# Seven tiles of k and q loaded eight tokens to a packet and turned by products, a first mask added by TensorE, and priorities by kind of work

## The chip, the cores and the metric

The kernel runs on one core of one Trainium2 chip. Its time is the device time of one execution in microseconds (us), the median of several runs. A core has five engines that matter here: PE (TensorE, products; PEld is its weight load), DVE (VectorE), ACT (ScalarE), POOL (GpSimd) and SP (SyncE, which here only issues transfers). Sixteen DMA engines move data between memory (HBM) and the on-chip SBUF. Products are written to PSUM, which has eight banks.

## The reference

Attention with four sink tokens and a window of 128, and a gated feed-forward network over its result:

```python
def _attn_ref(q, k, v, n_sink, window):          # q, k, v: (4, 8, 768, 64) float32; n_sink 4, window 128
    scores = np.matmul(q, k.transpose(0, 1, 3, 2)) / np.sqrt(D)
    keep = (pos[None, :] < n_sink) | ((rel >= 0) & (rel < window))     # rel = query - key
    scores = np.where(keep, scores, -1e9)
    a = softmax(scores)
    return np.matmul(a, v)

def _moe_ref(x, w_gate, w_val, w_out, rms_g):    # x: 3072 tokens x 512; d_ff 1536
    xn = x / np.sqrt(np.mean(x * x, axis=-1, keepdims=True) + 1e-6) * rms_g
    g = xn @ w_gate
    return (g * sigmoid(g) * (xn @ w_val)) @ w_out                     # float32
```

x is the attention's output with the eight heads side by side in a row of 512.

## The kernel before

**Tiles.** The 4 x 768 tokens are 24 tiles of 128 tokens, six to a batch; tile `bt` has index `t` within its batch. For each tile k, q and v (256 KB each in float32) are loaded by three transfers issued on SP (`load`, L415) into a ring of nine buffers `st`. A partition holds one token, and each of its eight heads is a run of 64 floats, 256 bytes, in memory. `casts` makes bfloat16 of them (`so` for k and q, with the scale in q's; `V` for v). `qk_unit` turns k and q, so that the head dimension lies on the partitions (`KQT`): for tiles 0 to 11 by four PE transposes of 128x128 for each tensor and a copy out of PSUM (L471, L476), from tile 12 on by a DMA transpose. On the first tile of a batch it also copies the sinks' k (`KS`), and on the others it makes the scores with the sinks (L491).

**Visits.** A tile has two visits of four heads (`visit`). The scores (L545, four products of 64 rows) go to a pair of banks, or two single ones; DVE masks them there, takes the negated maximum (L587), and ACT takes four exponentials (L591). On a batch's first tile the mask is a predicated copy of -1e30 over the keys after the query (L558, `m_first`, `negbig`); on other tiles the older tile's scores are copied over the current tile's where the window has moved on (L567, `m_old`), and the sinks' scores are put beside them (L578, and L597 and L601 for their exponentials). The weights are turned by PE (L609, the first twelve visits) or by DMA transposes, POOL splits them into the current and the older tile's part (L625, L629), and products with V follow (L638 for the sinks, L646, L651), with a reciprocal (L662) and the division into `x` (L665) on DVE.

**Rows and network.** `rows` normalizes a tile (ACT L675, POOL L677, L680 and L683, DVE `xr` L323) and turns it (`xnt`: PE L696 for the first tiles, then DMA transposes). `f_unit` makes a gate product and a value product (L721, sixteen matmuls of 128 columns for the first four tiles and the last two, which stand alone; eight of 256 for the others, which go in pairs, each unit then covering two column blocks), a tanh on ACT (L735), and two DVE products (`p` L739, `h` L742). `o_unit` makes the output (L753, twelve matmuls of 512 columns in three parts), copied by ACT (L764) and stored by SP (L767).

**Weights.** Nine transfers of 512 KB in bfloat16, read as float32 from memory, are issued by POOL: gate and value columns in three parts each (L441, g0 to g2 and v0 to v2), then the output weights (L447). `FIRST` gives their order and earliest time in the plan. The first of them waits until k of tile 1 has landed (`HOLD`).

**Order.** Nothing is left to a scheduler at run time. `Plan.order` simulates all operations with the written costs and due times, takes at each step the one that can start first and, among those, the one of lowest rank, chooses engine and bank for it, and the kernel is written out in that order for each engine (`add_manual_dep`). Every engine works in its order, so an instruction that waits holds up all behind it on its engine. `room` adds some slack after `ROOM_FROM` between an operation's end on one engine and its use on another. Attention runs up to `LEAD` = 12 visits ahead of the network. Where the plan has gaps on PE before 38 us, `Plan.fill` puts in products of a blank tile (L819), each reckoned at 0.109 us, whose result nobody uses.

Of the kernel before, what the change touches and what calls it, by code (L numbers as in the profile page):

```python
# [9 lines left out]
ALU = mybir.AluOpType  # L10
ACT = mybir.ActivationFunctionType
AX = mybir.AxisListType
FP32 = mybir.dt.float32
# [14 lines left out]
FFRANK = 1000.0  # L28
QK_DMA = 12
FIRST = "g0:2 v0:10 g1:13 v1:18 g2:20 v2:27 o1:38 o2:39 o0:39"  # L30
SHARES = {"SP": 0.2, "POOL": 0.95}
ROOM = {"PE": 0.6, "DVE": 0.2}
ROOM_FROM = 70.0
# [25 lines left out]
class Plan:  # L59
# [10 lines left out]
    def op(self, alts, fn, reads=(), writes=(), rank=0.0, takes=None, banks=(), after=()):  # L70
        o = Op(alts, fn, rank)
# [18 lines left out]
    def dma(self, queue, issue, moves, fn, reads=(), writes=(), rank=0.0, lag=1.1, after=()):  # L90

        o = self.op([(queue, issue, issue)], fn, reads=reads, rank=rank, after=after)
# [15 lines left out]
    def order(self):  # L108
# [59 lines left out]
        while len(done) < len(self.ops):  # L168
            pick = None
            for o in ready:  # L170
# [9 lines left out]
                key = (s, o.rank)  # L180
                if pick is None or key < pick[0]:
                    pick = (key, o, c, a)
            t = event()
            if t is not None and (pick is None or t <= pick[0][0]):
# [49 lines left out]
def kernel(  # L234
# [72 lines left out]
    def evac(n):  # L307
        return on(DVE=0.09 + 0.47e-3 * n, ACT=on_act(n))
# [32 lines left out]
    negbig = const.tile([P, 1], FP32, name="negbig")  # L341
    m_old = const.tile([P, P], I16, name="m_old")
    m_first = const.tile([P, P], I16, name="m_first")
# [33 lines left out]
    def c_masks():  # L377

        for m in (m_old, m_first):
            nc.gpsimd.memset(m, 1)  # L380
            nc.gpsimd.affine_select(
                out=m, in_=m, compare_op=ALU.is_gt, fill=0,
                base=0, pattern=[[1, P]], channel_multiplier=-1,
            )
        nc.gpsimd.memset(m_first[:, 0:NS], 0)

    def c_small():
        nc.vector.memset(negbig, NEG)
        nc.vector.memset(nhalf, -0.5)
        for i in range(2):  # L390
            nc.vector.memset(KS[i], 0.0)
        for i in range(10):
            nc.vector.memset(V16[i][:, :, D:D + 1], 1.0)
# [6 lines left out]

    plan.op(on(POOL=0.8), c_ident, writes=["ident"], rank=-3000)
    plan.op(on(DVE=0.6), c_small, writes=["small", ("KS", 0), ("KS", 1)] + [("V", i) for i in range(10)], rank=-3000)
    plan.op(on(ACT=1.4), lambda: nc.scalar.activation(out=warm, in_=nhalf, func=ACT.Exp), reads=["small"], rank=-3000)
    plan.op(on(POOL=1.4), c_masks, writes=["masks"], rank=-2999)
    plan.op(on(DVE=1.2), c_sinks, writes=[("VS", 0), ("VS", 1)] + [("PK", i) for i in range(NPS)], rank=-2999)

# [3 lines left out]
    def load(bt, rank):  # L410

        b, t = divmod(bt, NT)
        for i, src in enumerate((k, q, v)):
            n = (3 * bt + i) % len(ST)
            LOADED[bt, i] = plan.dma("SP", 0.45, 1.33, lambda src=src, n=n: nc.sync.dma_start(  # L415
                out=ST[n], in_=src[b, :, t * P:(t + 1) * P, :].rearrange("h t d -> t h d"),
            ), writes=[("ST", n)], rank=rank + 0.1 * i,
                after=VISIT[2 * bt - PACE:2 * bt - PACE + 1] if 2 * bt >= PACE else [])

    def casts(bt, rank):  # L420

        for i, nm in enumerate("kqv"):
# [12 lines left out]
            plan.op(alts, fn, reads=[("ST", n)], writes=[key], rank=rank + 0.1 * i)  # L435

    def load_w(nm, i, rank):
# [3 lines left out]
        return plan.dma("POOL", 0.78, 3.1 if c1 - c0 > 256 else 1.8, lag=1.5, fn=lambda: nc.gpsimd.dma_start(  # L441
# [3 lines left out]
    def load_wo(part, rank):  # L445
        f0, f1 = 4 * part, 4 * part + 4
        return plan.dma("POOL", 0.78, 3.1, lag=1.5, fn=lambda: nc.gpsimd.dma_start(  # L447
# [5 lines left out]
    def qk_unit(b, t, rank):  # L453
# [6 lines left out]
        if bt >= QK_DMA:  # L460
            plan.dma("SP", 1.2, 1.6, lambda: nc.sync.dma_start_transpose(
                out=KQT[par][:, t].rearrange("c a h p -> c (a h) p"), in_=SO[m].rearrange("p a d -> p (a d)")),
                reads=[("SO", m, 0), ("SO", m, 1)], writes=[("k", par, t), ("q", par, t)], rank=rank)
        else:
            for i, nm in enumerate("kq"):
                bk = Banks(ONES)

# [7 lines left out]
                o = plan.op(on(PE=0.23), tr, reads=["ident", ("SO", m, i)], takes=bk, rank=rank + 0.1 * i, after=after)  # L475
                plan.op(evac(HP * P), lambda e, bk=bk, i=i: copy(  # L476
# [405 lines left out]
```

## Time and profile before

| | us |
|---|---|
| median of 3 runs | 266.91 (266.44 to 267.27) |
| the profiled execution | 267.78 |
| its span, first to last instruction | 266.0 |
| mean granted TensorE clock | 0.999 |

| engine | busy us | share | instructions |
|---|---|---|---|
| PE | 254.8 | 96% | 2685 |
| PEld | 190.1 | 71% | 2702 |
| DVE | 211.0 | 79% | 510 |
| ACT | 147.3 | 55% | 419 |
| POOL | 140.0 | 53% | 272 |

HBM was read at 28.57 MB and written at 6.29 MB; the sixteen DMA engines moved 41.83 MB in 129155 packets, 121312 of them under 512 bytes.

How to read it: the span is cut into 40 slices, and each digit of a slice is the busy share of it in tenths. A group of instructions is given with its line, engine, operation, tiles written and read, count, busy time, mean duration of one in ns, and behind the bar the idle time of its engine just before them and what ended it. Matmuls overlap in the array, so the mean duration of one is longer than the distance between two starts. In windows, each engine's busy time in a stretch is followed by its instruction count, and the last three numbers are the granted clock, the DMA share and GB/s. The chain is the work that ended last, followed back from the end.

### The profile page before, as it was taken

What the parts mean: (1) busy time and instruction counts of PE and PEld (TensorE: products, weight loads), DVE (VectorE), ACT (ScalarE), POOL (GpSimd) and SP (SyncE); (2) the same over time, 40 slices, a digit from 0 to 9 for tenths busy, and PEclk for the clock granted to TensorE, in tenths of its full rate; (3) what the DMA queues carried; (4) which work ended last, traced back from release to release, by engine and by line L of the source; (5) the groups of instructions that cost most, each with busy time, mean ns of one, the idle gap of its engine ahead of it and who ended that gap; (6) DMA issues with size and microseconds to landing.
All of it is one profiled execution on the core that took longest, in us unless ns stands there. A gap on an engine that the chain in (4) does not pass through costs nothing.

```text
span 266.0 us, 7200 instructions
## 1 busy us (share of the span) xinstructions
PE 254.8 (96%) x2685; PEld 190.1 (71%) x2702; DVE 211.0 (79%) x510; ACT 147.3 (55%) x419; POOL 140.0 (53%) x272
## 2 busy tenths in 40 slices
PE   8998998999998999999999999999999999999994
PEld 6686877865666857858758668587587686785981
DVE  3977699999989898988959959679689599494641
ACT  2463676867767647456645467356664555551430
POOL 3566646579446897563637645734534446243100
PEclk9999999999999999999999999999999999999999
DMA  8999999979999989999999969969792431412311
GB/s 162 214 182 210 209 209 199 204 157 233 209 170 165 199 170 187 163 246 192 216 148 240 172 119 226 173 165 179 158 195 40 92 86 25 123 28 46 101 42 39
DMA packets 129155, 41.83 MB, mean 157 GB/s; under 512 B 121312, under 2 KB 125920, under 8 KB 129120
## 3 DMA queue, kind: packets, MB, share of 16 engines
q1 hardware_dynamic: 124368, 36.65, 75.2%
q0 software_dynamic: 4752, 4.72, 10.9%
q8 instruction: 21, 0.34, 0.6%
q14 instruction: 14, 0.11, 0.1%
HBM read 28.57 MB, written 6.29 MB: 131 GB/s over the span
## 4 chain that ended last, share of the span: by engine, by line
PE 81%; DVE 10%; DMA 5%; issue 2%; ACT 1%; POOL 0%; POOLq 0%
PE one L721 45%; PE one L753 22%; DMA wg_bf<-in_moe_w_gate_dram 5%; PE pair L545 4%; PE one L819 3%; DVE nmax L587 3%; PE one L646 2%; PE one L651 2%; PE one L638 1%; PE one L471 1%; DVE one L567 1%; PE one L609 1%; DVE h L742 1%; DVE so L323 1%; DVE x L665 1%
## 5 line engine op out<-in xcount | busy, mean ns | idle before, releaser
L721 PE MATMUL one<-xnt,wg_bf 128*128 128x256 bf16 (+1 forms) x720 | 72.0, 251 | 1.7 <-DMA wg_bf<-in_moe_w_gate_dram 1.0
L721 PE MATMUL one<-xnt,wv_bf 128*128 128x256 bf16 (+1 forms) x720 | 72.2, 251 | 0.3 <-DMA wv_bf<-in_moe_w_val_dram 0.2
L753 PE MATMUL one<-wo_bf,h 128*128 128x512 bf16 x271 | 68.1, 379 | 0.9
L735 ACT ACTIVATE th<-one 128x512 bf16<-128x512 f32 x72 | 42.7, 602 | 42.3 <-PE one L721 35.0
L721 PEld LDWEIGHTS <-wg_bf 128*128 128x128 bf16 x720 | 57.4, 98 | 10.5 <-issue 2.0
L721 PEld LDWEIGHTS <-wv_bf 128*128 128x128 bf16 x720 | 57.3, 98 | 9.7 <-issue 3.2
L739 DVE SCALAR_TENSOR_TENSOR p<-th,one 128x512 bf16<-128x512 bf16 x72 | 48.3, 677 | 15.1 <-ACT th L735 14.8
L591 ACT ACTIVATE ps<-pair,nmax 128x128 bf16<-128x128 f32 x152 | 43.7, 370 | 16.5 <-DVE nmax L587 8.6
L742 DVE TENSOR_TENSOR h<-p,one 128x512 bf16<-128x512 bf16 x72 | 48.3, 679 | 3.3 <-PE one L721 2.1
L753 PEld LDWEIGHTS <-h 128*128 128x128 bf16 x288 | 25.7, 98 | 26.3 <-issue 2.5
L683 POOL TENSOR_TENSOR xg<-x,grow 128x512 bf16<-128x512 bf16 x24 | 27.9, 1165 | 29.5 <-DVE x L665 27.1
L625 POOL TENSOR_SCALAR_AFFINE_SELECT cur<-pt 128x512 bf16<-128x512 bf16 x40 | 25.6, 639 | 29.5 <-DMA pt<-ps 21.5
L764 ACT ACTIVATE osb<-one 128x512 f32<-128x512 f32 x24 | 14.4, 599 | 24.0 <-PE one L753 23.8
L587 DVE TENSOR_REDUCE nmax<-pair 128x4 f32<-128x528 f32 (+1 forms) x38 | 26.5, 696 | 0.5
L567 DVE COPY_PREDICATED pair<-m_old,pair 128x512 f32<-128x512 int16 x32 | 22.0, 688 | 5.0 <-PE pair L545 4.0
L629 POOL TENSOR_SCALAR_AFFINE_SELECT old<-pt 128x512 bf16<-128x512 bf16 x40 | 25.8, 644 | 0.1
L597 POOL TENSOR_TENSOR sd<-sk,nmax 128x16 f32<-128x16 f32 x40 | 8.9, 224 | 25.7 <-DVE nmax L587 23.3
L665 DVE TENSOR_TENSOR x<-one,rden 128x256 bf16<-128x256 f32 x48 | 20.0, 417 | 0.5
L675 ACT ACTIVATE sq<-x 128x512 bf16<-128x512 bf16 x24 | 15.2, 634 | 9.2 <-DVE x L665 7.2
L819 PE MATMUL one<-blank 128*128 128x256 bf16 x132 | 19.2, 295 | 1.2 <-POOL blank L370 1.2
L662 DVE RECIPROCAL rden<-one 128x4 f32<-128x4 f32 x48 | 8.4, 176 | 10.8 <-PE one L651 9.4
L819 PEld LDWEIGHTS <-blank 128*128 128x128 bf16 x132 | 13.4, 106 | 3.8 <-POOL blank L370 1.2
(73 smaller groups left out, 305.2 us busy)
## 6 DMA issues: line engine op xcount, KB each, us to landing
st<-in_k_dram SPq DMA_DIRECT2D x24, 256.0 KB, 4.6
st<-in_q_dram SPq DMA_DIRECT2D x24, 256.0 KB, 4.9
st<-in_v_dram SPq DMA_DIRECT2D x24, 256.0 KB, 5.1
out_dram<-osb SPq DMA_DIRECT2D x24, 256.0 KB, 2.9
wg_bf<-in_moe_w_gate_dram POOLq DMA_DIRECT2D x3, 512.0 KB, 10.5
wv_bf<-in_moe_w_val_dram POOLq DMA_DIRECT2D x3, 512.0 KB, 9.2
wo_bf<-in_moe_w_out_dram POOLq DMA_DIRECT2D x3, 512.0 KB, 10.6
pt<-ps SPq DMA_TRANSPOSE x36, 3.3
```

Of the source, the lines that this page charges most:

```text
L567: nc.vector.copy_predicated(out=ap[:, :, P:2 * P], mask=m_old.unsqueeze(1).to_broadcast((P, hs.stop - hs.start, P)), data=ap[:, :, 0:P],)
L587: nc.vector.tensor_reduce(out=nm[:, hs], in_=ap[:, :, c0:2 * P], axis=AX.X, op=ALU.max, negate=True)
L591: plan.op(on(ACT=0.253), lambda h=h: nc.scalar.activation(out=PSM[r3][:, h, :], in_=head(h)[:, P:2 * P], func=ACT.Exp, bias=nm[:, h:h + 1] ...
L625: plan.op(on(POOL=0.6), lambda: nc.gpsimd.affine_select(out=cur, in_=PTT[r3][:, 0:4, :], compare_op=ALU.is_ge, fill=0.0, base=0, pattern=[ ...
L629: plan.op(on(POOL=0.6), lambda: nc.gpsimd.affine_select(out=old, in_=PTT[r3][:, 0:4, :], compare_op=ALU.is_gt, fill=0.0, base=0, pattern=[ ...
L683: plan.op(on(POOL=1.05), lambda: nc.gpsimd.tensor_tensor(out=xg, in0=X16[r], in1=grow, op=ALU.mult), reads=xs + ["g"], writes=[("XG", bt % ...
L721: nc.tensor.matmul(out=bank(bk)[:, i * n * P:(i + 1) * n * P].rearrange("p (t c) -> p t c", c=P), lhsT=w[:, kt, ft * P:(ft + 1) * P], rhs= ...
L735: plan.op(on(ACT=0.49), lambda: nc.scalar.activation(out=th, in_=b3(gb), func=ACT.Tanh, scale=0.5), banks=[gb], after=[o], writes=[("TH", ...
L739: plan.op(on(DVE=0.6), lambda: nc.vector.scalar_tensor_tensor(out=p1, in0=th, scalar=1.0, in1=b3(gb), op0=ALU.add, op1=ALU.mult,), banks=[ ...
L742: plan.op(on(DVE=0.6), lambda: nc.vector.tensor_tensor(out=HT[g % len(HT)][:, f0:f1, 0:n * P], in0=p1, in1=b3(vb), op=ALU.mult,), banks=[v ...
L753: nc.tensor.matmul(out=bank(bk)[:, 0:DM], lhsT=h[:, ft, tb * P:(tb + 1) * P], rhs=wo_bf[:, ft, :], start=(ft == 0), stop=(ft == FTN - 1),)
L819: done = plan.fill(done, lambda: nc.tensor.matmul(out=ONE[-1][:, 0:256], lhsT=blank[:, 0:P], rhs=blank, start=True, stop=True), 0.109)
```

## The change

1. **Loads.** For tiles 0 to 6 (`WIDE = 7`) k and q are loaded with partition (h, a) holding eight consecutive tokens of head h, 8 x 64 floats, 2 KB to a packet; v stays as it was.
2. **Turning.** For these tiles each tensor is turned by sixteen products with half of the identity's columns, 64 columns each, into a float32 bank (L515 of the new file), and copied out of it with the tokens put back in order (DVE or ACT).
3. **First mask.** `m_first` becomes a bfloat16 tile of 0 and -1e30. On a batch's first tile PE writes it to the scores' banks by two products with the identity (L605), and the scores' products add to it; the predicated copies of L558 and `negbig` are gone. The masks are made by two POOL steps in place of one.
4. **Priorities.** Each operation is given a kind. `place` shifts its rank by `SHIFT`, and by `EARLY` too for early ones; the network's operations have ranks of half their number plus `FEED`. In the plan loads get earliest times (`BEGIN`), weights another order and other times (`FIRST`), the slack is smaller but holds from 40 us on and for all engines, ACT may take an operation of lower rank that starts up to 0.05 us later before 20 us, and the plan's transfer cost of a load is 0.75 or 1.2 in place of 1.33.

In the orders that result, PE has 56 fillers in place of 132, DVE 476 instructions in place of 509; ten of the fourteen turned copies are on ACT; POOL copies more of V; and the first loads on SP are k, q of tile 0, q of tile 1, v of tile 0, k of tile 1.

```diff
+WIDE = 7
-FIRST = "g0:2 v0:10 g1:13 v1:18 g2:20 v2:27 o1:38 o2:39 o0:39"
+FIRST = "g0:5@4 v0:8@5 g1:10@2 v1:20@3 g2:19@6 v2:22@7 o1:37@0 o2:39@1 o0:45@8"
-ROOM = {"PE": 0.6, "DVE": 0.2}
-ROOM_FROM = 70.0
+ROOM = {"PE": 0.3, "DVE": 0.1, "ACT": 0.1, "POOL": 0.4, "SP": 0.1}
+WINDOW = {"ACT": 0.05}
+WINDOW_TO = 20
+SHIFT = {
...
+EARLY = {
...
+FEED = {"gate": 1000, "tanh": 9, "val": 14, "p1": 4, "h": 8, "out": 1000, "out_copy": 1000, "store": 1000}
+BEGIN = {(0, 2): 2, (1, 0): 2, (5, 2): 13, (6, 1): 23, (6, 2): 25, (7, 0): 25, (8, 1): 37, (9, 2): 48}
+ROOM_FROM = 40.0
...
+    def place(self, kind, rank):
+        if rank < -900:
+            return rank
+        if kind in FEED:
+            return (rank - FFRANK) / 2 + FEED[kind]
+        return rank + SHIFT.get(kind, 0.0) + (EARLY.get(kind, 0.0) if rank < 16 else 0.0)
...
-            LOADED[bt, i] = plan.dma("SP", 0.45, 1.33, lambda src=src, n=n: nc.sync.dma_start(
-                out=ST[n], in_=src[b, :, t * P:(t + 1) * P, :].rearrange("h t d -> t h d"),
+            wide = bt < WIDE and i < 2
+            LOADED[bt, i] = plan.dma(f"load_{i}", "SP", 0.45, 0.75 if wide else 1.2, lambda src=src, n=n, wide=wide: nc.sync.dma_start(
+                out=ST[n].rearrange("p j d -> p (j d)") if wide else ST[n],
+                in_=src[b, :, t * P:(t + 1) * P, :].rearrange("h (a j) d -> h a (j d)" if wide else "h t d -> t h d", **({"j": H} if wide else {})),
...
+                def turn(i=i, bk=bk):
+                    for j in range(H):
+                        for r in range(2):
+                            nc.tensor.matmul(
+                                out=bank(bk)[64 * r:64 * r + 64, 64 * j:64 * j + 64], lhsT=SO[m][:, i, D * j:D * j + D],
+                                rhs=ident.rearrange("p (g r a) -> p r g a", g=HP, r=2)[:, r], start=True, stop=True,
+                                skip_group_check=True,
+                            )
+                if bt < WIDE:
+                    o = plan.op("turn", on(PE=0.5), turn, reads=["ident", ("SO", m, i)], takes=bk, rank=rank + 0.1 * i, after=after)
+                    plan.op("turn_out", on(DVE=0.6, ACT=on_act(DM)), lambda e, bk=bk, i=i: copy(
+                        e, KQT[par][:, t, i].rearrange("c g (a j) -> c j g a", j=H),
+                        bank(bk).rearrange("c (j g a) -> c j g a", j=H, g=HP)),
+                        banks=[bk], after=[o], writes=[(nm, par, t)], rank=rank + 0.1 * i)
+                    continue
...
+        def m_mm():
+            for hs, ap in parts():
+                for i in range(0, hs.stop - hs.start, 2):
+                    nc.tensor.matmul(
+                        out=ap[:, i:i + 2, P:2 * P], lhsT=ident, rhs=m_first.unsqueeze(1).to_broadcast((P, 2, P)),
+                        start=True, stop=False, skip_group_check=True,
+                    )
+        if t == 0:
+            first = plan.op("mask_mm", on(PE=0.22), m_mm, takes=sb, reads=["ident", "first"], after=after + VISIT[-1:], rank=rank)
...
-                        start=True, stop=True,
+                        start=(t > 0), stop=True, skip_group_check=(t == 0),
...
-        if t == 0:
-            def mask():
-                for hs, ap in parts():
-                    w = hs.stop - hs.start
-                    nc.vector.copy_predicated(
-                        out=ap[:, :, P:2 * P], mask=m_first.unsqueeze(1).to_broadcast((P, w, P)),
-                        data=negbig.unsqueeze(2).to_broadcast((P, w, P)),
-                    )
```

## The prediction

> **What bounds the kernel now.** I read the page's slices first, then groups by form, then windows, and last the chain and the PE timeline of 19 to 45 us. The page says that PE is full:
>
> ```profile
> span 266.0 us, 7200 instructions
> PE 254.8 (96%) x2685; PEld 190.1 (71%) x2702; DVE 211.0 (79%) x510; ACT 147.3 (55%) x419; POOL 140.0 (53%) x272
> PE   8998998999998999999999999999999999999994
> DMA  8999999979999989999999969969792431412311
> PEclk9999999999999999999999999999999999999999
> ```
>
> PE is above 0.8 everywhere, but part of that does nothing: the plan fills its gaps before 38 us with products of a blank tile, 132 of them in all. The groups by form price them, and what the change touches:
>
> ```profile
> L819 PE MATMUL one<-blank 128*128 128x256 bf16 x132 | 19.2, 295 | 1.2 <-POOL blank L370 1.2
> L471 PE MATMUL one<-ident,so 128*128 128x128 bf16 x96 | 9.2, 223 | 1.3 <-DVE p L739 0.6 <-DVE so L323 0.5
> L558 DVE COPY_PREDICATED_SCALAR pair<-m_first,negbig 128x512 f32 x6 | 4.4, 738 | 0.1
> L558 DVE COPY_PREDICATED_SCALAR one<-m_first,negbig 128x256 f32 x4 | 1.7, 478 | 0.0
> ```
>
> The windows, of all engines, say where the span is lost (PE busy is the third number):
>
> ```profile
> 0.00:19.56 19.56, 17.68 (x166) 13.60 (x167) 13.44 (x55) 8.60 (x26) 10.10 (x29) 1.00 1.05 186
> 19.56:24.90 5.34, 4.10 (x67) 3.21 (x67) 3.86 (x11) 1.00 (x3) 3.00 (x6) 1.00 1.23 211
> 24.90:45.00 20.10, 18.86 (x291) 16.74 (x292) 17.10 (x44) 13.54 (x38) 12.91 (x23) 1.00 1.11 202
> 45.00:90.00 45.00, 42.85 (x548) 31.61 (x546) 43.03 (x121) 33.92 (x102) 28.60 (x57) 1.00 1.14 191
> 90.00:250.00 160.00, 159.37 (x1483) 115.95 (x1492) 127.77 (x275) 86.69 (x247) 85.40 (x161) 1.00 0.80 149
> ```
>
> The same windows for L819 alone give 14.46, 0.28 and 4.42 us of filling in the first three. So PE's time without real work is 16.3 us before 19.56 (1.88 idle, 14.46 filling), 1.5 to 24.90, 5.7 to 45, 2.2 to 90, 0.6 to 250, and 4.0 at the end, 30.3 together; 235.7 us are real. From 90 us on nothing but PE's work sets the time. The loss lies before 45 us, where the chain names the second gate weights:
>
> ```profile
> 12.79 12.07 DMA wg_bf<-in_moe_w_gate_dram
> 24.90 1.07 PE one L721 x16
> 25.97 2.18 PE one L819 x20
> ```
>
> and the timeline shows PE standing there, with filling behind:
>
> ```profile
> 19.56 1.05 PE L721 MATMUL one<-xnt,wg_bf 128*128 128x128 bf16 x16
> 24.90 1.07 PE L721 MATMUL one<-xnt,wg_bf 128*128 128x128 bf16 x16 [1.04 <-DMA wg_bf<-in_moe_w_gate_dram]
> 38.11 1.26 PE L819 MATMUL one<-blank 128*128 128x256 bf16 x10
> ```
>
> So the lever is the moment t2 when the second gate product starts (24.90), and how much attention work PE has behind it by then.
>
> **The change, part by part.** *Loads.* The hardware queue alone moved 1.05 MB in 5 to 10 us: 1.25 us for 256 KB in packets of 256 bytes. The price of 2 KB packets is bounded by two rows: 1.25 (no gain), and the weights' queue, whose packets read 2 KB and were busy 93% of the 16 engines for 750 packets in 15 to 20 us, 99 ns each, so 128 / 16 x 99 ns = 0.8 us. I take 0.8, since packet size is what they share: 0.45 us less for each of fourteen loads. The stalls of SP in its queue (7.98 and 6.43 us at 12.96 and 21.03) should go, as a wide load puts 128 packets there instead of 1024; who was late behind them were casts of tiles 3 and 4.
>
> *Weights.* POOL's first weights follow the VS copy, which needs v of tile 0. That load is now fourth, behind three wide ones: 3 x 0.8 + 1.25 = 3.7 us of transfers, as before (3 x 1.25). The cast of it waits less on DVE (7.37 before, some 6.6 now), so the first gate weights are issued at about 8.3 instead of 9.11. From that issue to the landing of the second gate weights before took 15.8 us, with 1.1 MB of loads beside (10 to 25 us), 4.2 loads; two thirds wide saves 2.8 x 0.45 = 1.3. So they land at about 8.3 + 15.8 - 1.3 = 22.8; with more of the loads done already, 21.5.
>
> *Attention ahead of the first gate.* k of tile 0 lands about 0.4 us earlier, at 3.6. From there to the first xr the new DVE order holds 37 instructions (six casts, three turned copies, five maxima, four masks and so on), 14.2 us by the rows; DVE's instructions start 0.08 us before the one ahead ends, so some 11.8. With 1.2 to 3 us of waits, as in this trace, xr comes at 16.6 to 18.4 (18.05 before), the first gate 1.3 later, and the second 3.1 after that (two units of 0.9, two of L646/L651 at 0.35, scores 0.33, two fillers): 21.0 to 22.8. Both sides agree, and t2 = 22.5.
>
> *What PE has done by t2.* Counting both orders at the trace's spacing (a tensor of L471 0.22, scores 0.33, or 0.22 on a first tile, L609 0.28 or 0.22, products with V 0.35 or 0.13, a unit of L721 0.9): before, six tensors, four scores, four of L609, four products with V and two units, 7.3 us (7.0 by the windows without L819 and idle time). After, at the old prices: eight, eight, five, five and two, 9.1. So 1.8 us of later work is gone by t2.
>
> *Turning by products.* A turned tensor is 16 products of 64 columns for 4 of 128. L646/L651, of 65 columns, start 0.030 us apart, so 0.48; at best two halves of the array run at once (0.24); at worst each waits for its weight load, 98 ns, 1.57. To this comes the change of shape: four scores take 0.33 us at 256 columns and 0.22 at 128, so 0.11 of each group is fixed. By 0.030, the nearest row, and half of the fixed part, 0.55, or 0.33 more than 0.22. Eight fall before t2, where PE waits anyway; six behind it cost 2.0 us.
> The Trainium skill speaks against this form: its page TensorEngine Tiling (Array Packing), Key Properties, says that a change of tiling mode drains the engine, and its Restrictions (Tile-to-Partition Mapping) that column tiling does without fast weight load. By the whole 0.11 at each turned tensor the six would cost 2.2; the trace agrees in that 0.11.
>
> *The first mask.* Two products of 256 columns, 0.22 us a visit at the 0.109 of L721 (16 in 1.74); two visits lie in the gaps, six cost 1.3. DVE loses 6.1 us of L558; 1.6 of them stood at 7.90 to 9.43 on the chain, which is within t2. If the gaps were gone, the first two would cost 0.44. The mask now waits on POOL's m_first, done at about 2.7 us in this trace, and behind it in PE's order stand only fillers and the first turned tensor, whose k lands at 3.6.
>
> *Filling behind t2.* The new order has 56 fillers, ten of them behind the second gate; before, 36 (4.42 us). Ten are 1.3: 3.1 less. This holds only where the work that the plan puts there is ready.
>
> *Queues and copies.* DVE has 33 instructions fewer; ten of the fourteen turned copies and most copies of xnt are ACT's (0.59 for 0.41 us on DVE). ACT was busy 75% in 45 to 90 us and hides them; uncovered, the two on tile 0's way cost 0.4, counted in the waits above. Behind 45 us the relief of DVE could return at most the 2.2 us idle there; the new priorities may as well lose as much. I take 0, with 1 us either way, and none at the end, whose last units stand in the same order.
>
> *Sum.* t2 - 24.9 - 1.8 + 2.0 + 1.3 - 3.1 = t2 - 26.5: -4.0 us at t2 = 22.5. The profiled execution took 267.78, 1.78 around its span, so 263.8 for one like it; the median of the runs is 0.87 lower, 266.91, and gives **262.9**. 0.3% (0.8 us) is about what a measurement of this kernel can tell from no change.
>
> **Rivals.** *The loads gain nothing* (2 KB packets cost as many bytes): g1 still lands at 24.9, t2 - 26.5 = -1.6, 265.3. For it: the 0.8 is another queue's. Against it: that queue reads 2 KB in 99 ns on the same engines. Chance 0.15.
>
> *The weights come later than before.* Place: the DMA engines from 10 to 25 us. In 15 to 20 us the loads got 0.16 MB beside 0.74 MB of weights, packet against packet of an eighth of the size; wide loads have packets as large. If they take as many turns, six wide and three narrow loads pass, 6 x 0.8 + 3 x 1.25 = 8.6 us for 5.3 before, and t2 = 24.1 + 3.3 = 27.4, +0.9, and about 0.5 again at the next weights: 268.3. It decides from t2 = 26.5 on. Against it: the first wide loads are through before the weights start. Chance 0.15, of which 0.03 within 0.3%.
> The Trainium skill (DMA: Bandwidth & Descriptors, Queues, rings and completion order) states this rule: each engine changes rows at packet boundaries. The trace agrees in that 0.16 to 0.74.
>
> *Turning costs the weight load*, 1.57: six behind t2 cost 8.1 for 2.0, eight before it push t2 to about 24.9: +4.5, 271.4. Against it: 30 ns between L646 and L651, which also load weights each time. Chance 0.05.
>
> *The priorities lose the gain behind 45 us* (3 to 4 us of new gaps; 0.05 now in any 10 us): no change, 0.03.
>
> **Chances.** The forecast has the other 0.62; its own range, with t2 from 21.0 to 24.9 and the 1 us, is 259.5 to 265.5. Faster 0.62 + 0.15 = 0.77, same 0.06, slower 0.17. The range over all, 259.5 to 267.6, leaves out the slower cases and 0.03 below.
>
> **What would show it.** Right: gate weights used from 18 us, the second gate at 21 to 24; fillers 56 and about 8 us; turned tensors 0.5 to 0.6 apart; SP without issues of several us; PE idle behind 45 us still 7 us with the end. Wrong: a DMA wait of 2 us or more at L784 of the new kernel before 30 us, PE holes behind 45 us, or a turned tensor near 1.5.

## The result, and the profile after

The changed kernel took 284.08 us (median of 4 runs, 283.90 to 286.27) beside 267.09 us of the kernel before (4 runs on the same chip): a ratio of 1.065, 95% interval 1.0586 to 1.0714. It is 17 us slower where 4 us less was forecast, and outside the range. A run that took over 1.5% more than the fastest of its kernel is left out of the medians and ratios of this document.

The page of the changed kernel, its head, PE's row of busy time, and four rows of slices:

```profile
span 282.1 us, 7421 instructions
PE 259.5 (92%) x2791; PEld 192.4 (68%) x2810; DVE 208.5 (74%) x475; ACT 170.9 (61%) x433; POOL 141.7 (50%) x279
PE   5677779969999999999999999999999999999994
ACT  3868895899699565664746546544665465452430
PEclk9999997987999999999999999999999999999999
DMA  4899699599819999798897788987897342322210
```

PE, full in the first slices before (filling included), now has gaps up to the ninth slice (about 60 us). ACT, a side engine before (0.55), is busy 0.8 or more in most of them, and the granted clock falls behind the gaps. The windows, of all engines:

```profile
0.00:20.00 20.00, 13.07 (x152) 8.07 (x153) 11.39 (x40) 11.31 (x17) 6.88 (x22) 1.00 0.79 187
20.00:45.00 25.00, 18.67 (x256) 13.93 (x255) 17.84 (x44) 21.58 (x47) 13.57 (x26) 0.97 0.97 199
45.00:90.00 45.00, 41.03 (x594) 32.57 (x595) 35.26 (x90) 38.12 (x90) 28.78 (x56) 0.90 0.83 154
```

The first two windows of the kernel before:

```profile
0.00:20.00 20.00, 18.12 (x173) 14.04 (x174) 13.79 (x55) 8.60 (x26) 10.52 (x30) 1.00 1.06 186
20.00:45.00 25.00, 22.52 (x353) 19.51 (x351) 20.61 (x53) 14.54 (x40) 15.50 (x27) 1.00 1.13 204
```

PE's 13.07, 18.67 and 41.03 stand against 18.12, 22.52 and 42.85 before; from 90 to 250 us it is 158.64 for 159.37, so the loss is again before 90 us. All filling (13.1 us by its group, 19.16 before) lies ahead of 45 us. Real work of PE by 45 us is therefore 13.07 + 18.67 - 13.1 = 18.6 us, where the kernel before had done 18.12 + 22.52 - 19.16 = 21.5: it is behind, though it has more to do.

Part of this busy time is slow work that the printed clock does not show: it stands at 1.00 up to 20 us, but the products of the filling, all of one form, take 421 ns in the changed kernel up to 29.8 us and 272 behind that (minimum, median and maximum in ns, then the first and last start):

```profile
L882 PE MATMUL one<-blank x41: 374/421/421, 1.2 to 29.7; 128*128 128x256 bf16 x41
L882 PE MATMUL one<-blank x14: 269/272/283, 30.3 to 40.4; 128*128 128x256 bf16 x14
```

Their starts stand 0.21 us apart at first and 0.11 later. In the kernel before, the short products begin at 5.6 us. What the slow stretch costs was not measured by itself.

What fills ACT is in the groups by form (copies of the products out of PSUM, on either engine; the last two lines are of the kernel before):

```profile
L350 ACT CAST KQT<-one 128x512 bf16<-128x512 f32 x10 | 23.9, 2541 | 6.0 <-PE one L515 6.0
L352 DVE CAST KQT<-one 128x512 bf16<-128x512 f32 x4 | 9.7, 2436 | 0.7 <-PE one L515 0.7
L315 ACT COPY KQT<-one 128x512 bf16<-128x512 bf16 x10 | 5.8, 585 | 2.9 <-PE one L471 2.9
L317 DVE COPY KQT<-one 128x512 bf16<-128x512 bf16 x14 | 5.7, 411 | 1.8 <-PE one L471 1.8
```

One turned copy takes 2.44 to 2.54 us; the copies that they replace took 0.585 and 0.411. Fourteen cost 33.6 us of engine time, where the prediction's prices (ten at 0.59 and four at 0.41) give 7.5. The chain up to 42 us goes through them (its pieces on these copies, and the first load):

```profile
0.80 4.08 DMA st<-in_k_dram
6.07 4.72 ACT KQT L350 x2
11.97 2.34 DVE KQT L352
14.62 2.35 DVE KQT L352
19.00 4.71 ACT KQT L350 x2
31.26 2.46 ACT KQT L350
39.23 2.44 ACT KQT L350
```

These copies are 19 of the first 42 us. The first gate products come last, and no weights are waited for any more:

```profile
34.40 1.07 PE L784 MATMUL one<-xnt,wg_bf 128*128 128x128 bf16 x16
37.56 1.05 PE L784 MATMUL one<-xnt,wg_bf 128*128 128x128 bf16 x16
```

Before, these stood at 19.56 and 24.90.

### The profile page after: what moved, and what is told of

Same layout as the page of the kernel before. It is cut to its first block, busy times and chain, and to the rows that moved or that the text cites. A ratio compares the mean times of both kernels' runs of the same rounds, so it can differ in the third digit from the quotient of the medians.

```text
span 282.1 us, 7421 instructions
## 1 busy us (share of the span) xinstructions
PE 259.5 (92%) x2791; PEld 192.4 (68%) x2810; DVE 208.5 (74%) x475; ACT 170.9 (61%) x433; POOL 141.7 (50%) x279
## 3 DMA queue, kind: packets, MB, share of 16 engines
q0 software_dynamic: 4752, 4.72, 10.6%
## 4 chain that ended last, share of the span: by engine, by line
PE 76%; ACT 10%; DVE 7%; DMA 3%; issue 2%; SPq 1%; DVEq 0%
PE one L784 42%; PE one L816 20%; ACT KQT L350 8%; PE pair L617 4%; PE one L709 2%; DVE KQT L352 2%; PE one L714 2%; DMA st<-in_q_dram 2%; DMA st<-in_k_dram 1%; PE one L701 1%; DVE nmax L650 1%; PE one L515 1%; DVE p L802 1%; PE one L532 1%; ACT ps L654 1%
## 5 line engine op out<-in xcount | busy, mean ns | idle before, releaser
L784 PE MATMUL one<-xnt,wg_bf 128*128 128x256 bf16 (+1 forms) x720 | 74.3, 257 | 0.7 <-ACT KQT L350 0.7
L784 PEld LDWEIGHTS <-wg_bf 128*128 128x128 bf16 x720 | 59.9, 101 | 9.3 <-issue 2.1
L654 ACT ACTIVATE ps<-pair,nmax 128x128 bf16<-128x128 f32 x156 | 46.9, 374 | 19.2 <-DVE nmax L650 14.8
L650 DVE TENSOR_REDUCE nmax<-pair 128x4 f32<-128x528 f32 (+1 forms) x39 | 27.3, 701 | 1.5 <-PE pair L617 0.9
L350 ACT CAST KQT<-one 128x512 bf16<-128x512 f32 x10 | 23.9, 2541 | 6.0 <-PE one L515 6.0
L630 DVE COPY_PREDICATED pair<-m_old,pair 128x512 f32<-128x512 int16 x33 | 22.7, 687 | 3.1 <-PE pair L617 3.0
L738 ACT ACTIVATE sq<-x 128x512 bf16<-128x512 bf16 x24 | 15.3, 636 | 16.0 <-DVE x L728 15.9
L660 POOL TENSOR_TENSOR sd<-sk,nmax 128x16 f32<-128x16 f32 x40 | 8.7, 220 | 18.4 <-DVE nmax L650 16.6
L617 PE MATMUL pair<-KQT 64*128 64x256 bf16 (+1 forms) x156 | 15.6, 281 | 2.4 <-ACT KQT L350 1.8
```

The source lines that it names most:

```text
L350: nc.scalar.copy(out=out, in_=in_)
L617: nc.tensor.matmul(out=head(2 * hi + hp)[:, (P if t == 0 else 0):2 * P].rearrange("p (g c) -> p g c", c=P), lhsT=QT[par][rows, t, 2 * half ...
L650: nc.vector.tensor_reduce(out=nm[:, hs], in_=ap[:, :, c0:2 * P], axis=AX.X, op=ALU.max, negate=True)
L654: plan.op("exp", on(ACT=0.253), lambda h=h: nc.scalar.activation(out=PSM[r3][:, h, :], in_=head(h)[:, P:2 * P], func=ACT.Exp, bias=nm[:, h ...
L784: nc.tensor.matmul(out=bank(bk)[:, i * n * P:(i + 1) * n * P].rearrange("p (t c) -> p t c", c=P), lhsT=w[:, kt, ft * P:(ft + 1) * P], rhs= ...
```

## The experiments

Times are medians; each ratio is to the kernel before on the same chip.

### The copies

**In the order of the bank.** The changed kernel's copy walks the bank in order and scatters on the write side: neighbouring elements go 8 places apart, 16 bytes in bfloat16. Swapping the sides puts the step on the read:

```diff
-  e, KQT[par][:, t, i].rearrange("c g (a j) -> c j g a", j=H),
-  bank(bk).rearrange("c (j g a) -> c j g a", j=H, g=HP)),
+  e, KQT[par][:, t, i].rearrange("c g (a j) -> c (g a) j", j=H),
+  bank(bk).rearrange("c (j x) -> c x j", j=H)),
```

> The changed kernel with one edit: the copy of a turned tensor out of PSUM goes through the tokens in their final order, so that it writes 512 neighbouring bfloat16 and reads float32 at a step of 64 elements; before the edit it read neighbours and wrote 2 bytes at a step of 16. Same instructions in the same order on every engine. Theory A (the scattered writes cost the time): the copies fall from 2.45 us (ACT) and 2.43 us (DVE) to 0.55 to 0.75 us, and the kernel from 284 to 262 to 268 us. Theory B (the float32 bank or the products that fill it make the copy slow): the copies stay above 2 us and the time at 284. Theory C (late loads and weights are the loss, the copies are hidden): the copies fall, the time stays above 276.

276.91 us (274.0 to 277.95), ratio 1.0321 (1.0236 to 1.0405). The copies are short again:

```profile
L350 ACT CAST KQT<-one 128x512 bf16<-128x512 f32 x10 | 5.8, 591 | 7.4 <-PE one L515 7.4
L352 DVE CAST KQT<-one 128x512 bf16<-128x512 f32 x4 | 2.8, 689 | 1.1 <-PE one L515 1.0
```

The step is free on the read side and dear on the write side. Some 9 of the 17 us are left (6 to 11 by the interval), more than the first theory allowed.

**The converse in the kernel before.** Its fourteen corresponding copies, of bfloat16 from PSUM, walk both sides in the scattered order, so the same values go to the same places.

> The kernel before, with the same fourteen copies (k and q of tiles 0 to 6, out of bfloat16 banks) made to go through their elements in the order of the changed kernel's copies, eight tokens apart, on both sides; the values end where they did, and the order of instructions is that of before. Theory A: these copies rise from 0.41 and 0.58 us to about 2.4, and the kernel from 267 by 8 to 18 us. Theory B: they stay under 0.8 us and the time under 269. If the copies rise and the time by less than 4 us, long copies by themselves do not explain the 17 us.

293.31 us, ratio 1.0957 (1.091 to 1.1003), with copies of 2.40 to 2.80 us; that is 26 us more, beyond the 8 to 18 expected. Nothing else of the change is in this kernel, so the copies alone are enough to cost more than the whole change did.

**The price by itself.** Behind the work of the kernel before, each copy of 512 elements a partition and each form of load was run twice alone.

> The kernel before, with work added behind its end that nothing uses (so its time is not compared): each copy of 512 elements twice on DVE and on ACT, from a float32 bank to neighbours, to the scattered order, in order with a read at a step, to a step of 2, 4 and 8 elements of bfloat16, to a step of 4 elements of float32; from a bfloat16 bank and from float32 in SBUF to the scattered order. Then sixteen products of 64 columns into neighbouring columns of a bank and into columns eight apart; then one load of k at a time in the old form, with the heads outermost and with the runs outermost, and four of each in a row. Theory A: all copies that write 2 bytes at a step of 16 bytes take about 2.4 us whatever their source, the read at a step 0.5 to 0.75. Theory B: the copies from the float32 bank take 2.4 us in any order. Theory D: a load with heads outermost takes about 1 us longer than one with runs outermost, and four of them about twice as long as four of these.

| copy of 512 elements a partition | DVE us | ACT us |
|---|---|---|
| float32 bank to neighbouring bfloat16 | 0.68 | 0.58 |
| the changed kernel's order | 2.45 | 2.43 |
| in token order, read at a step of 64 | 0.69 | 0.58 |
| bfloat16 written at a step of 2 | 0.72 | 0.73 |
| at a step of 4 | 1.29 | 1.29 |
| at a step of 8 | 2.42 | 2.42 |
| float32 written at a step of 4 | 1.29 | 1.40 |

A plain step of 8 costs what the changed kernel's order does, on both engines, and halving the step about halves the price down to a step of 2. From a bfloat16 bank the changed kernel's order took the same (2.42 and 2.43). From float32 in SBUF it took 2.45 on ACT but 1.30 on DVE, where 2.4 was expected: on DVE the price depends on the source too, and why stays open.

The same run had sixteen products of 64 columns, as they turn a tensor, with the output in neighbouring columns of a bank and eight columns apart: 0.25 us from the first start to the last, and 0.37. Moving the step from the copy to the products would have a price there.

The Trainium skill (SBUF — State Buffer, Door 1: The DMA port swizzle) has lines of 16 bytes in this memory, full bandwidth for consecutive accesses to one line when it gets two or more, and a free step of up to 8 bfloat16 or 4 float32 elements. The direction agrees, the limit does not: a step of 4 bfloat16, two elements to a line, took 1.29 us in place of 0.68 and 0.58.

### The loads

**Runs outermost.** On top of the copies in order, partition 8a + h takes the place of (h, a), so the slowest dimension of a load has sixteen runs and not eight heads; the half identity is read with the columns permuted to match.

```diff
-  "h (a j) d -> h a (j d)"
+  "h (a j) d -> a h (j d)"
-  rhs=ident.rearrange("p (g r a) -> p r g a", g=HP, r=2)[:, r]
+  rhs=ident.rearrange("p (a g r) -> p r g a", g=HP, r=2)[:, r]
```

> The kernel of e1_copy_in_order, and besides the wide loads put the sixteen runs of eight tokens outermost and the eight heads inside them (partition 8a + h in place of 16h + a); the products pick their columns of the identity accordingly. In the changed kernel the first wide load landed 4.08 us after its issue, later than the narrow one before (3.2 us), and five loads alone kept the sixteen DMA engines busy at 81%. Theory D (a load whose outermost dimension in memory is eight heads runs on eight engines only): the first load lands after 2.6 to 3.2 us and the time falls by 0.5 to 2 us against e1_copy_in_order. Theory E (a 2 KB packet takes that long on any engine): the first load still takes about 4.1 us, and the time is that of e1_copy_in_order within 0.3%.

270.87 us, ratio 1.0112 (1.0064 to 1.016). k of tile 0 lands 3.57 us from its issue, 4.08 in the changed kernel; 2.6 to 3.2 was expected. But a turned tensor now takes 1.05 us from its first start to the next instruction's: the products, which read 64 columns of the identity at a step of eight, start 54 ns apart. That was my own addition.

**Columns in a row.** Two DVE copies make the permuted identity once. I call this kernel the repaired one.

> The kernel of e2_loads_a_outer, with the identity's columns put into their new order once, by two small copies on DVE, so that the turning products stream neighbouring columns; in e2_loads_a_outer they streamed columns at a step and a turned tensor took 1.05 us, in e1_copy_in_order and the changed kernel 0.46 to 0.64. The rest of the order is the same. If that step was the cost, a turned tensor takes 0.5 us again and the kernel 3 to 6 us less than e2_loads_a_outer, 265 to 268 us. The rival that the late second gate weights (16.5 us from issue to landing in e2_loads_a_outer, 29.56 us for the second gate product) set the early part: the tensors fall to 0.5 us, the second gate product stays at 28 to 30 us, and the time falls by less than 3.5 us, 267 to 270.

268.26 us, ratio 1.0013 (0.9986 to 1.004): the kernel before again, and some 8 to 9 us less than with the copies alone mended. The products start 16 ns apart, and a turned tensor takes 0.37 to the next instruction, as it does with the copies alone mended; so this gain is the loads'. From 2 to 10 us the run with the copies alone mended (first) and the repaired kernel (second) differ in what the DMA engines move, the last two columns (the changed kernel, with the loads of the first, has 0.67 and 186):

```profile
2.00:10.00 8.00, 5.62 (x62) 3.44 (x63) 2.24 (x10) 1.45 (x4) 0.69 (x5) 1.00 0.67 187
2.00:10.00 8.00, 6.87 (x76) 3.94 (x77) 3.63 (x14) 2.17 (x6) 1.68 (x8) 1.00 1.07 229
```

The first gate product comes at 22.33 for 25.32. The loads by themselves point to the reason. In windows of the run with copies and loads by themselves, four narrow loads (first) and heads outermost (second) stand one behind another; the last two columns are the share of the 16 DMA engines and GB/s:

```profile
283.60:287.00 3.40, 0.00 (x0) 0.00 (x0) 1.89 (x2) 3.34 (x3) 0.00 (x0) 0.50 1.34 215
289.00:291.00 2.00, 0.00 (x0) 0.00 (x0) 0.00 (x0) 0.71 (x1) 0.00 (x0) 0.50 0.52 183
```

(A share over 1 means that packets overlap on an engine.) Narrow loads keep all engines busy; with heads outermost the share is 0.52, what eight busy engines of sixteen give. Alone such a load lands in 4.10 and 4.22 us, a narrow one in 3.20 and 3.06, runs outermost in 3.55. In a row, however, the four with runs outermost moved 193 GB/s (291.5 to 299.1 us), little more than the 183 above and not the double that was expected. The Trainium skill (DMA: Bandwidth & Descriptors, Why a DMA increments its semaphore by 16 and not by 1) says that a transfer gets the largest number of engines, up to 16, that divides the slowest dimension on both sides. For eight heads that is 8, and the 0.52 agrees.

**The repaired kernel with the scattered copy again.** One line differs from the repaired kernel.

> The kernel of e6_columns_in_a_row with the copies of the changed kernel (2 bytes at a step of 16). So only the copies are slow here, not the loads. Against e6_columns_in_a_row it gives the price of the scattered copies when the loads are in time: the changed kernel against e1_copy_in_order gave 6.7 us with late loads. If the two losses hide one another, it is 9 to 16 us above e6_columns_in_a_row; if they add up, 6 to 8.

284.17 us, ratio 1.0611 (1.058 to 1.0641), and copies of 2.555 and 2.434 us. With loads in order the copies cost 15.9 us; with the changed kernel's loads, 7 to 9 (284.08 to 276.91 by the medians, 1.065 to 1.0321 by the ratios). The loads cost 8 to 9 us with fast copies and nothing with slow ones (284.08 against 284.17). The two losses hide behind one another; either kept alone costs 8 us or more.

### The rest of the change

**Narrow loads under the new priorities** (`WIDE = 0`, so transposes turn all tiles, as before; the first mask stays with TensorE).

> The changed kernel with WIDE = 0: all k and q loaded in the old form and turned by four transposes; the first mask by TensorE, the priorities by kind and all plan numbers stay, and the plan orders the work anew. If the loads and the turning are the whole loss, it runs at 262 to 267 us. If the priorities or the mask lose too, it stays above 268.

277.29 us, ratio 1.0363 (1.03 to 1.0426), with 109 fillers.

**Wide loads under the old priorities**, with the loads and copies as repaired, in the kernel before.

> The kernel before, with only the loads and the turning of the change, in the form of e6_columns_in_a_row (runs outermost, sixteen products over a reordered identity, copy in order), reckoned by the plan at what they took (0.55 us for the products, 0.61 or 0.48 for the copy); priorities and masks as before. By the measured prices the loads gain nothing in time to land (3.55 us alone for 3.1), a little in the engines' time, and the turning costs PE 0.3 us for each of fourteen tensors: 266 to 270 us. If packets of 2 KB bring the gain that the prediction gave them, 262 to 265.

273.78 us, ratio 1.022 (1.0187 to 1.0254), with 108 fillers; 266 to 270 was expected. Either half alone is 6 to 10 us slower, together they are level: the halves' prices don't add. A changed half gives a whole new order on all engines, so these two tell that the numbers of the plan and the loads belong together, not what one is worth.

**The mask alone, in the kernel before.**

> The kernel before with the first mask alone changed: two products a visit put the mask into the bank ahead of the scores, and the vector engine's predicated copies (6.1 us) go. The prediction's price is +1.3 us for six visits behind the second gate product, less up to 1.6 us of the predicated copies that stood on the chain ahead of the first gate: 266.5 to 268.4. If the mask is part of what kept the repaired kernel from a gain, or holds PE up behind 45 us, 269 or more; if relief of the vector engine is worth more than its products cost, below 266.

269.19 us beside 267.49, ratio 1.0066 (1.0038 to 1.0095), +1.7 us. The order is a new one here too (116 fillers for 132). The second gate product came a little earlier (24.01 for 24.90), and PE lost it behind: 40.66 us busy from 45 to 90 for 42.85.

**The mask taken out of the repaired kernel**, in all batches and then in the last three.

> The repaired kernel (copies in token order, runs outermost loads, columns in a row) with the first mask made by the vector engine's predicated copies again, in all four batches. By the account of PE's work, the repaired kernel does about 5.9 us more products than the kernel before, 2.5 to 3 of them mask products; the mask alone cost the kernel before 1.7 us. If work on PE is what is left, the time falls by 1 to 2 us, to 266.3 to 267.3 beside 268.3, and with the other priorities around it may reach the kernel before or pass it. The rival: before 20 us DVE is the later engine, the predicated copies of the first batch push the first gate product behind 22.3, the fillers are more, and the time is 268.3 or more.

> As the run with no mask products, but the first batch, which falls where PE has gaps and DVE has none, keeps them; the other three batches use predicated copies. PE loses six visits of two products, 0.22 us each by the prediction's price, 1.3 us: 266.5 to 267.2, the best of the repaired kernels. The rival: DVE, busy over 40 of 45 us behind 45 us, takes the 0.6 us of each predicated copy onto PE's path, and the time stays at 268 to 269.

282.35 us (1.0518; 1.0474 to 1.0563) and 273.70 us (1.0223; 1.0188 to 1.0258). Both expected gains failed: with less work for TensorE both kernels were slower. With the mask products kept in the first batch alone, PE is busy 153.26 of the 160 us from 90 on, where the repaired kernel has 157.11. These two also have new orders (94 fillers in the first), so they don't price the mask; they show that taking its products out of this plan brought no gain.

### The weights

In the repaired kernel's timeline PE waits for the value weights and then the second gate weights:

```profile
22.33 1.07 PE L793 MATMUL one<-xnt,wg_bf 128*128 128x128 bf16 x16
25.66 1.07 PE L793 MATMUL one<-xnt,wv_bf 128*128 128x128 bf16 x16 [1.91 <-DMA wv_bf<-in_moe_w_val_dram]
28.75 1.65 PE L793 MATMUL one<-xnt,wg_bf 128*128 128x128 bf16 x16 [0.29 <-DMA wg_bf<-in_moe_w_gate_dram]
```

Weights are issued at 10.08, 11.07 and 12.09 us, and the last lands some 16.6 us later; before, it took 12.07 from its issue at 12.79.

**All weights earlier in the plan**, held only until k of tile 0 is in.

> The repaired kernel (copies in token order, runs outermost loads, columns of the identity in a row) with the first three weight loads no longer held until k of tile 1 is in and the VS copy is done, only until k of tile 0 is in; the weights are issued at about 5 to 7 us, not at 10.1 to 12.1. If the late second gate weights are what is left of the loss, they land at about 7 + 16.5 = 23.5 us, the second gate product starts at 24 instead of 28.75, and by the prediction's rule (a microsecond for a microsecond, from the 268.3 that the repaired kernel took) the time is about 264. The rival: the transfers are bound by their bytes, and what the weights gain the loads of tiles 1 to 3 lose; then k and v of tile 1 land some 3 us later, the first gate product is later than 22.3, PE has holes before 20 us that the filling does not cover, and the time is 268 to 272.

279.35 us, ratio 1.0436 (1.0382 to 1.0491). The second gate product came at 27.94 where 24 was expected, but the plan chose another order (103 fillers), so this tells little. The next four runs keep every engine's order and move one thing.

**Only the issue of the first weights moved**, on POOL ahead of the VS copy, in the repaired kernel (three) and in the kernel before (two). With it the first of them waits for q of tile 1 or of tile 0, no longer for k of tile 1.

```diff
+    vs_at = min(o.start for o in done if o.fn is not None and "vs_unit" in o.fn.__qualname__)
+    for n, o in enumerate(AHEAD_OF_VS):
+        o.start = vs_at - 0.1 + 0.01 * n
```

> The repaired kernel with every engine's order kept, but the first three weight loads (g0, v0, g1) put on the Pool engine's queue ahead of the first VS copy and held until q of tile 1 is in instead of k of tile 1; they are issued at about 7, 8 and 8.8 us for 10.1, 11.1 and 12.1, and VS starts at 9.5 for 8.9. By the prediction's rule (the moment of the second gate product is worth a microsecond for a microsecond), with g1 landing 16.5 us from its issue at 25.3, PE no longer waits there, the second gate comes at 25.5 to 26.5 for 28.75, and the time is 265.3 to 266.3 for 268.3, ahead of the kernel before. The rival, as in the kernel with all weights earlier: the loads of tiles 1 and 2 give way to the weights, the first gate product stays at 22.3 or later, and the time is 267.5 to 270.

> The kernel before, every engine's order kept, with its first two weight loads put ahead of the first VS copy on the Pool engine and held until q of tile 0 is in: issued at about 6 and 7 us for 9.11 and 10.10; the third, for the second gate product, stays behind VS and is issued at about 11 for 12.79. If the moment of the second gate product is what sets the time, as the prediction's sum had it, it comes 1 to 1.8 us earlier than 24.90 and the time is 265 to 266. If k and q of tiles 1 to 3 lose what the weights gain, the first gate product moves behind 19.6, holes come behind 38 us, and the time is 267 to 269.

270.87 us (1.0108; 1.0078 to 1.0139) and 275.46 us (1.0293; 1.0256 to 1.033). Both lie beyond their rival's range, and by its mechanism: the first gate products move back, to 29.41 and 26.64, since k, q and v come late (POOL waits 9.10 us for a v in the first, DVE 5.10 for a k in the second). PE in the repaired kernel with the weights ahead:

```profile
15.00:20.00 5.00, 1.92 (x23) 0.91 (x19) 3.02 (x12) 3.00 (x11) 0.00 (x0) 1.00 1.20 208
20.00:25.00 5.00, 2.11 (x28) 1.51 (x29) 1.43 (x4) 0.83 (x3) 2.88 (x6) 0.50 1.17 267
```

The DMA engines are full (1.20, 1.17), and PE stands for 6 of 10 us.

**The loads of tile 4 moved back instead**, behind the first gate weights and then behind the second ones, in the repaired kernel.

```diff
+    tc.add_manual_dep(
+        LOADED[(4, 0)].made, G0.made.name,
+        mybir.DependencyInfo(mybir.DependencyClass.Sync, mybir.DependencyReason.DATA),
+        reason="the first weights come before the later tiles",
+    )
```

> The repaired kernel with every engine's order kept, and k of tile 4 (and all loads behind it on the SyncE queue) held until the first gate weights have landed at about 20 us; it is issued at 14.6 in the repaired kernel and its cast comes at 27.4. If the loads that no longer stall in their queue are what makes the weights late, two loads of 256 KB fewer stand beside the weights before 20 us; at the 0.23 MB in 1 us that the DMA engines moved there that is up to 2.2 us: the first product with the value weights at 23.5 to 24.7 for 25.66, the second gate product at 26.5 to 27.5 for 28.75, and the time 266 to 267.3 for 268.3. The rival: k of tile 4 now lands behind 27.4, the turned tensors of tile 4 and what follows come later, PE has new holes from 30 to 45 us, and the time is 268.3 or more.

> As the kernel before it, but k of tile 4 and the loads behind it held until the second gate weights have landed. With the first hold (released at 21.2 us) the second gate product stayed at 28.8, with five loads issued beside it from 21.2 to 24.6. If these took the transfers, then without them the 0.7 MB of weights still outstanding at 21.2 take 3 us at 0.23 MB in 1 us; the second gate weights land at 24.3 to 25, k of tile 4 is issued then and cast at about 28, the second gate product starts at 25 to 26, and the time is 265 to 266.5. The rival: q of tile 4 and the tiles behind it come too late for the products from 30 to 45 us, which the hold moves by 3 us, and the time is 268 or more.

268.23 us (1.0033; 1.0009 to 1.0056) and 270.77 us (1.0129; 1.0102 to 1.0155). The first brings the value product 1.1 us earlier (24.52) and the second gate product nothing (28.77). The second brings that to 26.10, about as expected, and pays with a hole of 5.67 us:

```profile
26.10 1.07 PE L793 MATMUL one<-xnt,wg_bf 128*128 128x128 bf16 x16 [0.34 <-DMA wg_bf<-in_moe_w_gate_dram]
32.83 0.64 PE L524 MATMUL one<-perm,so 128*64 128x64 bf16 x16 [5.67 <-DVE so L352]
```

The cast that ends the hole, at 32.35, had itself waited 6.87 us for k of tile 4. So the loads of later tiles did take the transfers from the weights, and they are needed almost as soon: what the one gains the other loses. None of the kernels beat the kernel before.

## Why the prediction was wrong

**The step that failed** is the price of the turned copies, under "Queues and copies". "ACT's (0.59 for 0.41 us on DVE)" took the duration of copies with neighbouring elements on both sides for one that writes 16 bytes apart; the range "0 with 1 us either way" and the "0.4" on tile 0's way rest on it. Measured: 2.44 to 2.54 us a copy; the two on tile 0's way take 4.72 us, and the first scores come at 10.84 for 7.51 before. The order of the copy alone is worth 7 to 9 us in the changed kernel and 15.9 in the repaired one. The step on the write side is shown as the cause, by the copies alone and by three pairs of kernels that differ in these copies only. I had bounded a turned tensor on PE from three rows and the copy behind it from one, of another pattern; no rival covered it.

**Loads, 0.8 us each in place of 1.25: wrong, hidden behind the copies.** The weights' queue shared the packet size, not the number of engines. From 5 to 10 us the changed kernel moved 210 GB/s at a share of 0.81, the kernel before 210 at 1.21. Even with runs outermost a wide load alone lands in 3.55 us, not sooner than a narrow one. Beside other traffic the repaired kernel moved 234 GB/s from 5 to 25 us and the kernel before 203, which larger packets may explain; the orders differ as well.

**Weights, g0 issued at 8.3: wrong.** It was 11.72; VS waited for the cast of v, and that for a slower load. In the repaired kernel it was 10.08.

**t2 as the lever: wrong as a price, a microsecond for a microsecond.** In the changed kernel t2 was 37.56, and t2 - 26.5 gives +11 for the measured +17. In the repaired kernel t2 = 28.75 gives +2.3 for some +0.7. With t2 at 26.10 by holding tile 4 back, the repaired kernel took 2.5 us more, not 2.6 less: what PE has ready behind t2 counts as well.

**The rival "the weights come later than before"** (t2 27.4, 268.3, 0.15) is nearest to what remains once copies and loads are repaired: 28.75 and 268.26. That its time agrees is luck, as the sum gives 269.2 at t2 = 28.75. That later loads take the transfers from the weights is shown by holding tile 4 back until the second weights. "The loads gain nothing" holds for a wide load alone (3.55 us for 3.20 and 3.06), not for its t2 or its 265.3. The rival of weight loads was wrong, and the priorities behind 45 us can't be priced, as above.

**Turned tensor 0.55: too dear.** From its first start to the next product of another shape it takes 0.37 us, and 0.57 in the changed kernel's slow stretch up to 29.8 us; there is no pause for a weight load. The products start 16 ns apart in the mean where the price had 30, as those for the two halves of a bank start in pairs, 3 to 4 ns apart, a pair every 32. So six tensors cost some 0.9 us more than before at 0.22, not 2.0. The fixed part for a change of shape, 0.11 in the price's working, does show: 0.12 to 0.13 us pass from the last start to a product of another shape, 0.03 where the next tensor follows.

**The first mask 0.22 a visit: right as PE's time.** Two products start 0.21 to 0.22 us ahead of what follows them in the repaired kernel. In the kernel before the mask and the order that came with it cost 1.7 us (0.4 to 0.95%), where six visits were put at 1.3.

**Filling: 56 as foreseen, but 13.1 us, not about 8,** since 41 of them lie in the slow stretch. The ten behind t2 took 1.25 us, as reckoned, but the work that the plan put there was not all ready: PE stood 1.48 us behind 40.89. So the condition named there failed.

**The sum for the repaired kernel closes by windows of PE.** By 45 us its real work is 15.92 + 21.95 - 10.6 = 27.3 us for 21.5 before. It does 252.2 - 10.6 = 241.6 in all for 235.7, so the 6 us it is ahead are about the 6 us the change adds: mask products (3.5 us by their groups), turning (10.0 for 9.2), and work done at a clock of 0.93 from 20 to 45 us (an estimate: 7% of 21.95, 1.5). Idle time and real work behind 45 us agree to 0.3 us. In the sum I had added the new work behind t2 only, and let eight turned tensors and two masks vanish in gaps.

**The forecast's own range** takes off the 0.87 twice: t2 from 21.0 to 24.9 with 1 us either way gives 260.4 to 266.3 by the sum, not 259.5 to 265.5.

**Signs.** SP still stalled for 4.65, 4.08 and 3.16 us, shorter than before. PE holes behind 45 us appeared, as "wrong" foretold: 41.03 busy of 45. The wait for weights did not, since work arrived later still.

## What to carry to other kernels

A copy's price is that of its access pattern, here above all of the step on the write side: take it from a row with the same pattern, or run it alone, before a duration of the same shape is used. Look at which dimension stands outermost in a transfer: with eight heads there the share of the DMA engines was 0.52, and packets eight times as large did not make up for it (4.10 and 4.22 us for 3.20 and 3.06). Where the DMA engines were full, an earlier transfer was a later one somewhere else; count what is needed by when before moving one.

## What I had not expected of the hardware

Reading at a step of 64 float32 elements in PSUM costs nothing on either engine (0.69 and 0.58 us), while writing bfloat16 at a step of 8 takes some four times as long (2.42). Only DVE reading from SBUF did it in 1.30, in the changed kernel's order.

A matrix product's moving operand of 64 columns, read at a step of eight columns: starts 54 ns apart in the mean, 16 with neighbours. With the output eight columns apart in PSUM it was 25 for 16 (0.37 and 0.25 us for fifteen steps).

The granted clock fell to one half near stops of PE of very different length. In the run with the weights ahead it is 0.50 from 20 to 25 us, in and behind a stop of 5.93 us. In the repaired kernel it is 0.50 from 26.7 to 30.0 us, and the longest stop in the 20 us ahead of it was 1.91; in the changed kernel it is 0.50 from 43.7 to 47.0 us, where the longest in the 20 us ahead was 1.48. The Trainium skill (TensorE: Matmul & The Clock Gate, Part 1: The HAM clock gate) has it halved after an idle window of some 3.4 us. Only the first case has a stop that long.
